# TensorE picks the width of a mixture-of-experts layer by the expert's token count

## The chip, the cores and the metric

The kernel runs on one core of a Trainium2 chip. The metric is the device time of one execution in microseconds (us), and less is better. The engines are called as in the profile: PE is TensorE (PEld its weight load), DVE is VectorE, ACT is ScalarE, POOL is GpSimd, and SP is the queue that starts most of the DMAs.

## The reference

A delta-rule attention over 4 batches, 8 heads, 768 steps and 48 features gives 3072 token rows of 384 numbers. A gate sends each token to one of 8 experts, which is two matrix products with a ReLU between them:

```python
logits = x @ w_gate                      # 3072 x 8
expert_idx = np.argmax(logits, axis=1)   # one expert for each token
for e in range(E):
    xe = x[expert_idx == e]
    h = np.maximum(xe @ w1[e], 0.0)      # 384 -> 1024
    out[expert_idx == e] = gate_w[...] * (h @ w2[e])   # 1024 -> 384
```

With the reference's inputs (seed 0) the experts 0 to 7 get 401, 342, 407, 383, 373, 410, 399 and 357 tokens.

## The kernel before, in words

**Attention.** The tokens are worked on in 24 chunks of 128. It takes a little over half of the span and is not changed.

**Routing.** Behind each chunk, `emit_slots` (L451) gives each token a slot: `base` holds the next free slot of every expert. POOL writes the token's row into the buffer `xg` in HBM with an indirect DMA (L519). An expert owns 448 slots (`CAP`): three groups of 128 and a last group of 64. At two points of the program `base` is raised for all experts (L495 and L497): behind chunk 18 to at least slot 256, behind chunk 22 to at least slot 384. So the groups in front are complete early and can be loaded early, the last group of every expert always holds the tokens of the last two chunks, and some slots in front stay empty. An empty slot is a row of zeros, and its result is dropped when it is written out. The last two chunks go to a buffer of their own, `xt`, which `load_last` (L595) loads as `xs` and `add_last` (L859, on DVE) adds to the last group.

**Experts.** For each expert `tokens` (L862) loads the 448 rows and transposes them to features by tokens in three steps (L882 for the full groups, L883 for the last one). `ffn` (L886) runs the first layer in eight blocks of 128 hidden features. A block is nine matmuls with 448 moving columns (`first`, L619: weights and tokens are each split in a high and a low part, three products for each of three slices of 128 features). ACT and DVE turn a block into the high and the low part of the hidden layer (L622, L623), and PE has three PSUM buffers for blocks. The second layer is 24 matmuls with 384 columns for each full group (`second`, L629) and 16 for the last group (L916). ACT scales the result by the gate (L911), and POOL scatters it to the output (L632). Of expert 0 the first two groups are computed during the attention, so what is left of it has 192 columns.

**Order.** The instructions of each engine stand in the order in which the loop over `t` writes them (0 to 11 for each expert: eight blocks, then the groups 0, last, 1, 2). `TOK`, `TOK0`, `PC` and `PC0` say at which `t` a step of the next expert's tokens or of its weights is written. Each engine works through its own list and waits on semaphores; SP's DMAs and POOL's scatters are lists as well.

**End.** Tokens beyond 448 of an expert would go through a loop of blocks. Behind the last expert DVE counts these blocks (L954 to L966). Each engine reads the count into a register (L975), which also waits for PE and ACT, and branches past the loop, since the count is zero here.

## Time and profile before

| | us |
|---|---|
| median of 3 runs | 563.91 |
| lowest, highest | 562.20, 567.53 |
| the profiled execution: its time | 564.33 |
| the profiled execution: its span | 562.6 |

The profile shows one execution. Its span runs from the first to the last instruction; the run's time is 1.73 us longer. Times in the rows are us from the start of the span. Line numbers such as L619 are those of the kernel before; in the next section, instruction lists headed by "now" have those of the changed file.

### The profile page before, as it was taken

What the parts mean: (1) busy time and instruction counts of PE and PEld (TensorE: products, weight loads), DVE (VectorE), ACT (ScalarE), POOL (GpSimd) and SP (SyncE); (2) the same over time, 40 slices, a digit from 0 to 9 for tenths busy, and PEclk for the clock granted to TensorE, in tenths of its full rate; (3) what the DMA queues carried; (4) which work ended last, traced back from release to release, by engine and by line L of the source; (5) the groups of instructions that cost most, each with busy time, mean ns of one, the idle gap of its engine ahead of it and who ended that gap; (6) DMA issues with size and microseconds to landing.
All of it is one profiled execution on the core that took longest, in us unless ns stands there. A gap on an engine that the chain in (4) does not pass through costs nothing.

```text
span 562.6 us, 17239 instructions
## 1 busy us (share of the span) xinstructions
PE 495.2 (88%) x7091; PEld 449.2 (80%) x7091; DVE 366.1 (65%) x1343; ACT 267.1 (47%) x590; POOL 94.6 (17%) x116
## 2 busy tenths in 40 slices
PE   5765597889989688978998999999999999999991
PEld 3554486778878677867897989999999999999991
DVE  2999989899999999746543666272744535372311
ACT  1661165576767474747342454353534435353310
POOL 4040001122421223132202010202011010202011
PEclk7996699899999998989999899999999999999996
DMA  8949449765874843655421565473745445371000
GB/s 264 289 92 267 159 152 280 212 208 155 231 248 97 267 132 118 195 170 168 154 74 71 148 213 165 114 208 108 205 122 161 131 128 166 119 201 54 12 17 25
DMA packets 68497, 88.61 MB, mean 157 GB/s; under 512 B 26541, under 2 KB 55390, under 8 KB 68416
## 3 DMA queue, kind: packets, MB, share of 16 engines
q1 hardware_dynamic: 64960, 77.92, 47.7%
q0 software_dynamic: 3456, 9.57, 4.8%
q8 instruction: 56, 0.92, 0.7%
q14 instruction: 25, 0.20, 0.1%
HBM read 57.20 MB, written 24.37 MB: 145 GB/s over the span
## 4 chain that ended last, share of the span: by engine, by line
PE 64%; DVE 27%; issue 3%; ACT 2%; DMA 1%; POOL 0%; SPq 0%; DVEq 0%; ACTq 0%; POOLq 0%
PE h L619 22%; PE y L629 18%; DVE lw L325 8%; DVE tmp L318 8%; PE y L916 4%; PE yp L404 3%; PE ks L388 3%; PE yp L422 3%; PE xp L445 2%; DVE v_all L380 2%; PE pq L235 2%; PE ks L361 2%; DVE wt L331 2%; PE ku L413 1%; PE xt L882 1%
## 5 line engine op out<-in xcount | busy, mean ns | idle before, releaser
L629 PE MATMUL y<-w2h,hx 128*128 128x384 f32 x352 | 93.5, 340 | 0.0
L325 DVE TENSOR_TENSOR lw<-lw,tmp 128x84 f32<-128x84 f32 (+26 forms) x372 | 83.7, 265 | 0.3
L318 DVE TENSOR_TENSOR tmp<-lg,lw 128x84 f32<-128x84 f32 (+26 forms) x372 | 79.9, 254 | 0.3
L552 DVE TENSOR_TENSOR w2l<-w2r,w2h 128x768 fp32r<-128x768 f32 x32 | 31.2, 978 | 73.2 <-ACT w2h L551 73.2
L392 ACT COPY u<-ks 32x384 f32<-32x384 f32 x96 | 45.1, 470 | 51.7 <-PE ks L388 50.1
L632 POOL DMA_INDIRECT out_dram<-yo,idx x32 | 30.7, 958 | 227.1 <-ACT yo L911 170.5
L629 PEld LDWEIGHTS y<-w2h,hx 128*128 128x128 f32 x352 | 63.8, 188 | 0.9
L619 PE MATMUL h<-xh,w1h 128*128 128x448 f32 x168 | 61.4, 365 | 0.0
L619 PE MATMUL h<-xh,w1l 128*128 128x448 f32 x168 | 61.3, 365 | 0.0
L619 PE MATMUL h<-xl,w1h 128*128 128x448 f32 x168 | 61.3, 365 | 0.0
L629 PE MATMUL y<-w2l,hx 128*128 128x384 f32 x176 | 59.1, 336 | 0.0
L388 PE MATMUL ks<-v_all,wt 32*32 32x48 f32 x1536 | 27.7, 211 | 35.0 <-DVE v_all L380 29.3
L388 PEld LDWEIGHTS ks<-v_all,wt 32*32 32x32 f32 x1536 | 23.2, 111 | 40.3 <-DVE v_all L380 33.1
L623 DVE SCALAR_TENSOR_TENSOR hx<-h,hx 128x448 fp32r<-128x448 f32 (+1 forms) x64 | 36.9, 587 | 24.8 <-ACT hx L622 24.4
L246 POOL TENSOR_SCALAR_AFFINE_SELECT pm<-pm 128x1024 f32<-128x1024 f32 x24 | 31.1, 1297 | 126.0 <-ACT pm L245 126.0
L622 ACT ACTIVATE hx<-h 128x448 fp32r<-128x448 f32 (+1 forms) x64 | 32.2, 515 | 38.5 <-PE h L619 38.5
L911 ACT ACTIVATE yo<-y,gt 128x384 f32<-128x384 f32 x22 | 12.8, 581 | 73.7 <-PE y L629 59.3
L361 PE MATMUL ks<-st,kt 128*32 128x96 f32 x768 | 46.5, 260 | 0.7 <-issue 0.7
L519 POOL DMA_INDIRECT xg<-row,sli x22 | 23.7, 1075 | 99.9 <-DVE sli L512 54.9
L220 ACT COPY gg<-pg 128x512 f32<-128x512 f32 x48 | 25.8, 588 | 26.3 <-PE pg L235 26.3
L361 PEld LDWEIGHTS ks<-st,kt 128*32 128x32 f32 x768 | 34.9, 115 | 4.2 <-issue 1.3
L552 DVE TENSOR_TENSOR w1l<-w1r,w1h 128x1024 fp32r<-128x1024 f32 x24 | 29.5, 1230 | 7.9 <-ACT w1h L551 7.5
(159 smaller groups left out, 1003.2 us busy)
## 6 DMA issues: line engine op xcount, KB each, us to landing
w1r<-in_w_dram SPq DMA_DIRECT2D x24, 512.0 KB, 4.0
w2r<-in_w_dram SPq DMA_DIRECT2D x32, 384.0 KB, 3.6
kt<-in_kt_dram SPq DMA_DIRECT2D x24, 256.0 KB, 5.5
qt<-in_qt_dram SPq DMA_DIRECT2D x24, 256.0 KB, 5.2
xg<-zrow SPq DMA_DIRECT2D x7, 788.0 KB, 8.0
xr<-xg SPq DMA_DIRECT2D x7, 591.0 KB, 6.0
xn<-row SPq DMA_DIRECT2D x10, 394.0 KB, 5.7
ku<-in_kn_dram SPq DMA_DIRECT2D x20, 192.0 KB, 3.4
```

Of the source, the lines that this page charges most:

```text
L246: nc.gpsimd.affine_select(out=pm, in_=pm, compare_op=ALU.is_gt, fill=0.0, base=0, pattern=[[0, H], [1, C]], channel_multiplier=-1)
L318: nc.vector.tensor_tensor(out=x, in0=lg[:, r0:r1, c:c + 1].broadcast_to([128, r1 - r0, b - a]), in1=lw[:, c:c + 1, a:b].broadcast_to([128, ...
L325: nc.vector.tensor_tensor(out=lw[:, r0:r1, a:b], in0=lw[:, r0:r1, a:b], in1=x, op=ALU.subtract)
L361: nc.tensor.matmul(ks[32 * q:32 * q + 32, 2 * p:2 * p + 2, :], lhsT=kt_t[n % KTL][:, p, 32 * q:32 * q + 32], rhs=st_view(n % B, p), start= ...
L388: nc.tensor.matmul(ks[r, h, :], lhsT=tiles[n // B]["wt"][r, n % B * H + h, :], rhs=vn[r, h, :], start=True, stop=True, tile_position=(32 * ...
L392: nc.scalar.copy(out=uview(n)[r], in_=ks[r])
L552: nc.vector.tensor_tensor(out=lo, in0=src, in1=hi.bitcast(F32), op=ALU.subtract)
L619: nc.tensor.matmul(ps, lhsT=w[:, d, fs], rhs=x_[:, d], start=(n == 0), stop=(n == len(terms) - 1))
L622: nc.scalar.activation(out=hh, in_=ps, func=AF.Relu)
L623: nc.vector.scalar_tensor_tensor(out=hl, in0=ps, scalar=0.0, in1=hh.bitcast(F32), op0=ALU.max, op1=ALU.subtract)
L629: nc.tensor.matmul(ps, lhsT=h(f)[h_], rhs=w2[w][:, f, :], start=(n == 0), stop=(n == len(terms) - 1))
L632: nc.gpsimd.indirect_dma_start(out=out, out_offset=bass.IndirectOffsetOnAxis(ap=idx, axis=0), in_=yo, in_offset=None, bounds_check=N - 1, ...
```

## The change

`emit_slots` raises `base` for expert 0 alone, and the last two chunks go to `xg` as well; `xt`, `xs` and `add_last` are gone. For the other experts `base` is then a plain count. DVE makes from it a number for each expert: 0 (at most 384 tokens), 1 (at most 416) or 2. Behind the first layer of expert 0 PE loads the seven numbers into registers, and a nest of branches stands at each of the eight blocks and at the last group of the experts 1 to 7. The nest at a block leads to nine matmuls with 384, 416 or 448 columns; the nest at the last group leads past its 16 matmuls where the number is 0. The count of the overflow blocks moves ahead of expert 0, its register load and a drain of POOL into the last expert, and the last group of the last expert is scaled by DVE and ACT, half each.

```diff
@@ emit_slots
-        dst = xg if tb * B + b < NN - DEF else xt
...
-            V.scalar_tensor_tensor(out=base, in0=lim, scalar=float(128 * NG - CAP), in1=base, op0=ALU.add, op1=ALU.max)
+            V.tensor_tensor(out=base, in0=base, in1=jump[:, 1], op=ALU.max)
...
-            nc.gpsimd.indirect_dma_start(out=dst, out_offset=bass.IndirectOffsetOnAxis(ap=sli[:, j:j + 1], axis=0),
+            nc.gpsimd.indirect_dma_start(out=xg, out_offset=bass.IndirectOffsetOnAxis(ap=sli[:, j:j + 1], axis=0),
@@ load_last
-        xs = xp_.tile([128, ROW], F32, name=f"xs{e}", tag="xs", bufs=2)
         for a in range(2):
-            nc.sync.dma_start(out=xs[64 * a:64 * a + 64], in_=xt[e * CAP + NG * 128:e * CAP + NG * 128 + 64, :])
-        return xs
+            nc.sync.dma_start(out=XR[e][64 * a:64 * a + 64, NG], in_=xg[e * CAP + NG * 128:e * CAP + NG * 128 + 64, :])
@@ tokens
-        xs = load_last(e)
...
-        add_last(xr, xs)
@@ ffn
-            first(ps[:, c], W["w1"], (xh, xl), slice(f * 128, (f + 1) * 128))
+            for i in by_width(e):
+                w = WID[i]
+                first(ps[:, c.start:w], W["w1"], (xh[..., 0:w - lo], xl[..., 0:w - lo]), slice(f * 128, (f + 1) * 128))
...
+                if (e, g) == (E - 1, NG - 1):
+                    hw = DM // 2
+                    nc.vector.tensor_scalar(out=yo[:, hw:], in0=ps[:, hw:], scalar1=gg_, scalar2=None, op0=ALU.mult)
+                    nc.scalar.activation(out=yo[:, 0:hw], in_=ps[:, 0:hw], func=AF.Copy, scale=gg_)
...
-                for n, (w_, f) in enumerate(terms):
-                    nc.tensor.matmul(ps[0:2 * w], lhsT=h2[:, f], rhs=w_[:, f, :],
-                                     start=(n == 0), stop=(n == len(terms) - 1))
+                for i in by_width(e):
+                    for n, (w_, f) in enumerate(terms if i else ()):
+                        nc.tensor.matmul(ps[0:2 * w], lhsT=h2[:, f], rhs=w_[:, f, :],
+                                         start=(n == 0), stop=(n == len(terms) - 1))
@@ new, ahead of the loop over the experts
+    for i, w in enumerate(WID[:2]):
+        V.tensor_tensor(out=kind[:, i], in0=base, in1=lim, op=ALU.subtract)
+        V.tensor_scalar(out=kind[:, i], in0=kind[:, i], scalar1=float(w - CAP), scalar2=None, op0=ALU.is_gt)
+    V.tensor_tensor(out=kind_i, in0=kind[:, 0], in1=kind[:, 1], op=ALU.add)
...
+    def by_width(e):
+
+        if e == 0:
+            yield 2
+            return
+        with tc.If(KIND[e] < 1) as low:
+            yield 0
+        with low.Else():
+            with tc.If(KIND[e] < 2) as mid:
+                yield 1
+            with mid.Else():
+                yield 2
...
@@ in the loop over the experts
+            if e == 0 and t == KF:
+                for i in range(1, E):
+                    KIND[i] = nc.values_load(kind_i[0:1, i:i + 1], engines=[mybir.EngineType.PE], min_val=0, max_val=2,
+                                             skip_runtime_bounds_check_because="a sum of two comparisons")
...
+            if e == E - 1 and t == 7:
+                nblk = nc.values_load(tot[0:1, 0:1], min_val=0, max_val=NJ + E)
+                nc.gpsimd.drain()
@@ behind the last expert: the count (cnt, nb, cum, tot and six POOL fills) is gone from here
-    nblk = nc.values_load(tot[0:1, 0:1], min_val=0, max_val=NJ + E)
     OV = tc.If(nblk > 0)
```

PE now, first layer of expert 1, the joint between two copies of a block and the next nest. In the names, `h` is the block's PSUM buffer, `xh` and `xl` are the two parts of the tokens, `w1h` and `w1l` those of the weights. The row with 384 columns is the last of the first copy:

```order
L621 MATMUL h_5696<-xh_5822,w1l_5753 128x384
L947 UNCONDITIONAL_BRANCH
L950 COMPARE_AND_BRANCH
L621 MATMUL h_5696<-xh_5822,w1h_5752 128x416 [waits Activation_49]
L621 MATMUL h_5696<-xl_5823,w1h_5752 128x416
```

Where nine matmuls of 448 columns stood, three copies of nine stand one behind the other, with branches between them that lead on to the next block.

PE, second layer of expert 1, the last group, with the transposes of the next expert's tokens (`xt`) ahead of it. Before:

```order
L882 MATMUL xt_1_6110<-ident,xr_5936 128x128 [waits PE_49]
L882 MATMUL xt_1_6110<-ident,xr_5936 128x128 x2
L883 MATMUL xt_1_6110<-ident,xr_5936 128x64
L916 MATMUL y_3_6117<-w2h_5840,hx_5940 128x384 [waits DVE_49]
L916 MATMUL y_3_6117<-w2l_5841,hx_5940 128x384
```

And now:

```order
L879 MATMUL xt_1_6298<-ident,xr_5974 128x128 [waits PE_49]
L879 MATMUL xt_1_6298<-ident,xr_5974 128x128 x2
L880 MATMUL xt_1_6298<-ident,xr_5974 128x64
L947 COMPARE_AND_BRANCH
L947 UNCONDITIONAL_BRANCH [waits PE_49]
L950 COMPARE_AND_BRANCH
L926 MATMUL y_5697<-w2h_5862,hx_5978 128x384 [waits DVE_49]
```

On the empty path nothing stands but a branch, and ahead of it PE waits for its own semaphore (`PE_49`), that is, until its matmuls up to there are finished.

POOL, the end of the program. Before:

```order
L953 IOTA e_7854 128x8 [waits PE_49]
L958 IOTA thr 128x168
L968 MEMSET itr 128x1
L969 IOTA part 128x1
L971 IOTA wo_7876 128x3
L972 IOTA wo_7877 128x8
L632 DMA out_dram<-yo_2_7808,idx_0_7433 3072x384 [waits DMASW6_49,Activation_49]
L975 TENSOR_LOAD tot [waits DVE_49,PE_49,Activation_49]
L1074 COMPARE_AND_BRANCH
```

Now:

```order
L1002 TENSOR_LOAD tot [waits DVE_49]
L947 UNCONDITIONAL_BRANCH x6
L634 DMA out_dram<-yo_0_8903,idx_0_8375 3072x384 [waits DMASW3_49,Activation_49]
L634 DMA out_dram<-yo_3_8932,idx_0_8375 3072x384 [waits DMASW4_49,DVE_49]
L634 DMA out_dram<-yo_1_8973,idx_0_8375 3072x384 [waits DMASW5_49,Activation_49]
L634 DMA out_dram<-yo_2_9002,idx_0_8375 3072x384 [waits DMASW6_49,Activation_49]
L1111 COMPARE_AND_BRANCH
```

The fills are gone from between the last scatters, and the register load stands ahead of the last four. The engines that have no part in a nest each get one unconditional branch for it, as POOL's six here.

## Rows read from the trace of the kernel before

**Rows 1.** The page: busy us (share) and instructions; the queue of PE's code.

```profile
PE 495.2 (88%) x7091; PEld 449.2 (80%) x7091; DVE 366.1 (65%) x1343; ACT 267.1 (47%) x590; POOL 94.6 (17%) x116
...
q8 instruction: 56, 0.92, 0.7%
```

**Rows 2.** Chain that ended last, experts 2, 3 and 7: start us, us, what.

```profile
361.22 14.68 PE h L619 x72
375.90 0.33 PE xt L882 x3
376.23 0.20 PE xt L883
376.43 4.39 PE y L629 x24
380.82 0.33 PE xt L882 x3
381.15 0.20 PE xt L883
381.35 2.98 PE y L916 x16
...
384.86 8.52 PE y L629 x48
393.39 14.42 PE h L619 x72
...
535.92 4.18 PE y L629 x24
540.09 2.77 PE y L916 x16
```

**Rows 3.** Busy us (x) of PE, PEld, DVE, ACT, POOL; PE clock, DMA share, GB/s.

```profile
100.00:200.00 100.00, 86.88 (x2264) 76.65 (x2262) 93.90 (x457) 68.14 (x193) 22.93 (x20) 0.98 0.68 197
...
380.00:420.00 40.00, 40.00 (x220) 37.73 (x219) 19.40 (x30) 17.67 (x29) 5.72 (x6) 1.00 0.49 141
```

**Rows 4.** Timeline, the end: start us, us, engine, line, operation [idle before <-releaser].

```profile
550.85 0.34 PE L629 MATMUL y<-w2h,hx 128*128 128x384 f32 x1
551.27 0.14 POOL L953 IOTA e<- 128x8 f32 x1 [2.33 <-PE y L629]
551.28 0.58 ACT L911 ACTIVATE yo<-y,gt 128x384 f32<-128x384 f32 x1 [3.58 <-PE y L629]
...
551.44 0.17 DVE L954 TENSOR_TENSOR cnt<-base,e 128x8 f32<-128x8 f32 x1 [7.25 <-POOL e L953]
...
552.25 0.99 POOL L632 DMA_INDIRECT out_dram<-yo,idx  x1 [0.17 <-issue]
...
554.07 0.15 DVE L966 CAST tot<-cum 128x1 int32<-128x1 f32 x1
```

**Rows 5.** Timeline, expert 0's rest and the attention's last steps.

```profile
294.60 0.86 PE L388 MATMUL ks<-v_all,wt 32*32 32x48 f32 x16
...
306.27 0.97 POOL L519 DMA_INDIRECT xt<-row,sli  x1 [0.30 <-issue]
...
308.18 0.92 PE L619 MATMUL h<-xb,w1h 128*128 128x192 f32 x2 [0.41 <-ACT xb L551]
...
309.25 2.37 SPq L598 DMA_DIRECT2D xs<-xt  x4
...
311.12 0.36 DVE L623 SCALAR_TENSOR_TENSOR hx<-h,hx 128x192 fp32r<-128x192 f32 x1 [2.60 <-ACT hx L622]
...
319.59 0.49 PE L882 MATMUL xt<-ident,xr 128*128 128x128 f32 x3
320.01 0.27 PE L883 MATMUL xt<-ident,xr 64*128 64x64 f32 x1
```

**Rows 6.** DMA issues: queue, operation and count, KB each, median us to landing.

```profile
xs<-xt SPq DMA_DIRECT2D x16, 98.5 KB, 2.4
...
out_dram<-yo,idx POOLq DMA_INDIRECT x32, 2.6
```

**Rows 7.** As rows 3, around the start of expert 0's rest.

```profile
304.00:308.00 4.00, 2.53 (x21) 2.22 (x20) 1.21 (x8) 0.78 (x2) 1.94 (x2) 1.00 0.18 68
308.00:312.00 4.00, 3.82 (x17) 3.72 (x18) 0.72 (x2) 1.37 (x3) 0.00 (x0) 0.51 0.31 90
312.00:316.00 4.00, 4.00 (x25) 4.00 (x25) 2.08 (x4) 1.85 (x5) 0.00 (x0) 0.64 0.88 251
```

## The prediction, written before the changed kernel ran

> **What bounds the kernel now.** I read the page's first part, then the chain of waits behind 330 us, then the table of stretches, then the timeline of the end. The page gives PE 88% of the span, DVE 65% and ACT 47% [rows 1]; a share over the whole span does not say who is waited for. The chain does: through the experts it holds nothing but PE, one piece end to end with the next [rows 2]. An expert is 72 matmuls of the first layer (14.42 or 14.68 us), three sets of transposes, 24 matmuls of group 0, 16 of the last group and 48 of the groups 1 and 2, about 32 us. [...] So each us taken from PE there is a us of the span, until DVE or DMA, at half load, come into the way. Behind PE's last matmul (550.85 + 0.34 = 551.19 us) the end of the program takes 562.6 - 551.19 = 11.4 us: POOL's fills, the count on DVE to 554.22, then 8.4 us with no instruction that the profile shows, in which the register load, the branch and the closing barriers lie [rows 4].

> **Which way the branches go.** The tokens of an expert, from the reference, are also the values that the changed `base` holds for the experts 1 to 7, since these are no longer raised. 342, 383, 373 and 357 (experts 1, 3, 4, 7) are kind 0: 384 columns and no last group. 407, 410 and 399 (experts 2, 5, 6) are kind 1: 416 columns. Expert 0 is not branched.

> **A. Narrower first layer.** A matmul of 448 columns takes 14.42/72 = 200.3 ns (14.68/72 = 203.9 where the expert's number is even). One of 384 columns takes 4.18/24 = 174.2 ns in the last expert, 8.52/48 = 177.5 and 4.39/24 = 182.9 in a loaded one [rows 2]. The difference is at most 203.9 - 174.2 = 29.7 ns and at least 200.3 - 182.9 = 17.4. [...] That is 72 x 26 = 1.87 us for kind 0 and half, 0.94, for kind 1: 4 x 1.87 + 3 x 0.94 = 10.3 us (6.9 to 11.8).

> **B. The skipped last group.** Three times 2.98 us and once 2.77 [rows 2]: 11.7 us. On the empty path PE waits until its own transposes are finished, so it runs dry four times. What that costs no row shows. At least 0. At most 0.6: a transpose's 0.27 us [rows 5] from start to end, and the 0.30 that POOL took between two of its instructions with nothing to wait for [rows 5]. I take 0.3, the restart alone, since most of a transpose is hidden by the one behind it: 4 x 0.3 = 1.2 us back (0 to 2.4).

> **C. The branches.** There are 7 x 9 = 63 nests. Kind 0 runs one comparison and one jump, kind 1 two comparisons, a jump over the first copy and one over the third. They cost PE nothing if its sequencer is ahead. The small matmuls of the attention pass at 0.86/16 = 54 ns each [rows 5], so nine are handed over in 0.49 us or less, while nine of 384 columns run for 9 x 174 = 1.57 us: 1.1 us a block is free. And ahead of each expert's first transposes the sequencer has waits on DMAs to pass, ahead of the second set it has none of these; both sets take 0.33 + 0.20 us [rows 2]. An instruction that the sequencer handles alone left no mark on PE. Below nothing I see no reason for; the upper bound is a fetch of code at each jump, at the 2.4 us of the fastest DMA landing [rows 6], which is a rival below. I take 0 by the nearest row, the waits.

> The row on those waits says that control work is free. [...]

> **D. Seven register loads on PE** behind expert 0's first layer. Not in any row. At least 0, at most one round trip of 2.4 us, the fastest DMA landing [rows 6], since they stand one behind the other and PE still has queued matmuls of 192 columns. I take 0.

> **E. The end.** The 3.03 us from PE's end to the count (551.19 to 554.22) leave the path, and so does the register load behind it. What is late next is the last scatter: half the scaling on each of two engines saves about 0.2 us of ACT's 0.58, so it starts at about 552.0 instead of 552.25 and lands 2.6 us later [rows 4, 6], at 554.6 on the old clock. So the gain is the register load and the early branch, less 0.4 us. Bounds: nothing, and the 8.4 us without an instruction less the 2.6 us of that landing, 5.8. I take 2, from a load of the size of the 2.4 us landing.

> **F. What hides.** Gone are eight DVE adds, 16 loads of `xs` and eight fills of `xt`: nothing on the path, since PE never waits there [rows 2, 3]. Moved onto DVE ahead of expert 0's rest are five operations for the kinds and twelve for the count, at about 0.2 us each 3.8 us (the twelve took 551.44 to 554.22 [rows 4]). DVE is idle for 2.6 us up to 311.12 there [rows 5], so its first `hx` comes about 1 us late, and PE needs that buffer only at the fourth block, about 314; if that cover goes, 1 us. The last two scatters now also wait for expert 0's loads from `xg`, and all expert loads for both scatters, as `xs` did. SP's load of expert 1's rows comes two DMAs earlier in its list than before, with `xs` gone. The 63 plain branches on DVE, ACT, POOL and SP cost those lists little, and these engines have half their time free [rows 3].

> **The sum** is -10.3 - 11.7 + 1.2 - 2 = -22.8 us against the profiled execution: 564.33 - 22.8 = **541.5 us**. The median before, 563.91, is 0.4 us below that execution, within what runs differ. The kindest ends of all terms give 564.33 - 11.8 - 11.7 - 5.8 = 535.0, the worst 564.33 - 6.9 - 11.7 + 2.4 + 2.4 + 1 = 551.5.

> **Rivals.**

> *Slower: code is fetched at each jump.* [...] For: the queue of PE's code brought 56 packets for 0.92 MB, about 253 of PE's 14,182 instructions each (0.7% of 16 x 562.6 us over 56 is 1.1 us a packet) [rows 1]. At 2.4 us a jump, a kind-0 block takes 0.49 + 2.4 = 2.9 us instead of 1.57, a kind-1 block with two jumps 5.3 instead of 1.68: 32 x 1.3 + 24 x 3.6 = 128 us, and with the gain of 24 us (the sum without B's restarts) 564.33 - 24 + 128 = 668 us. It decides from about 1.1 us a jump on, where 24 x (0.49 + 2.2 - 1.68) = 24 us eat the whole gain. Against: a jump passes at most 18 matmuls with their weight loads and two branches, 38 instructions, so it stays in the packet or goes to the one behind it, which was due next. [...] Chance 0.10, most of it slower.

> *No change: a branch drains PE.* If each nest, and not the empty path alone, lets the array run dry, it costs 63 x 0.3 = 19 us: 564.33 - 24 + 19 = 559 us; at 0.6, 578. For: a register is compared, and nothing says what is held meanwhile. Against: the waits passed unseen in C. Chance 0.11.

> *The clock falls.* [...] Against: between 100 and 200 us PE rests 13% of the time in small pieces, and the clock stays at 0.98 [rows 3]; the new pauses are smaller and fewer. Chance 0.04.

> *The branch takes the wide path*, for counts other than those I worked out: only the end gains, 562 us. Chance 0.02.

> **How the numbers follow.** The forecast has 0.73. Its own range is 535 to 551.5; with the clock's case and part of a draining branch I give 535 to 555, which leaves out the fetch, the full drain and the wide path, under 0.2. A difference under 1% (5.6 us) can't be told from none. Faster by more: 0.73, the clock's 0.04 and a small part of the draining branch, 0.79. Same: most of the draining branch, the wide path and the fetch near its balance, 0.12. Slower: 0.09.

> **What would show it.** In the profile after: blocks of 72 matmuls of 12.5 us in the experts 1, 3, 4 and 7 and of about 13.5 in 2, 5 and 6; no matmuls of the last group in four experts; PE at 9 tenths and more through the experts, with a gap of about 0.3 us where the group is skipped; about 9.4 us from PE's last matmul to the end. I am wrong if PE shows gaps at the joints of the blocks that its sequencer is named for (C), if the gap at an empty group is 1 us or more (B), if PE stops at 315 to 320 for its registers (D), or if the end still takes 11 us (E).

## The result and the profile after

| | before | after |
|---|---|---|
| median of 4 runs each, us | 563.06 | 540.81 |
| lowest, highest | 559.93, 567.53 | 539.12, 543.51 |
| the profiled execution: time, span | 564.33, 562.6 | 543.51, 541.8 |

The ratio of the runs is 0.960 (95% interval 0.953 to 0.968): faster, by 22.2 us. The forecast was 541.5.

I cut both profiled spans at the same places: the start of expert 0's rest, its end, the start of the transposes behind it, PE's last end.

| stretch, us | before | after | difference |
|---|---|---|---|
| attention, up to expert 0's rest | 308.18 | 311.06 | +2.9 |
| expert 0's rest, first layer | 11.41 | 10.32 | -1.1 |
| pause of PE behind it | 0 | 1.31 | +1.3 |
| from there to PE's last matmul | 231.60 | 213.40 | -18.2 |
| from PE's last matmul to the end | 11.4 | 5.7 | -5.7 |
| span | 562.6 | 541.8 | -20.8 |

The first two lines can't be put down to the change. Attention's code is nearly the same, yet in 14 profiled executions of the kernels of this study expert 0's rest began anywhere from 303.45 to 316.00 us, in the two with the old layout at 308.18 and 308.15, and the rest itself took 10.3 to 11.8. So kernels are compared below by the stretches behind it.

The page (as [rows 1]):

```profile
PE 481.1 (89%) x7027; PEld 440.0 (81%) x7027; DVE 361.9 (67%) x1341; ACT 268.2 (49%) x590; POOL 96.1 (18%) x119
...
q8 instruction: 66, 1.08, 0.8%
```

PE runs 64 matmuls less, the four empty groups, and ten packets of code more, the copies.

The first layers of the experts 1 to 7 after, one stretch each (from:to, length, busy us and count of PE, then of PEld, clock, DMA share, GB/s), matmuls of the first layer alone:

```profile
331.80:345.00 13.20, 13.04 (x72) 12.35 (x72) 1.00 0.75 247
360.00:374.00 14.00, 13.72 (x72) 13.47 (x72) 1.00 0.69 199
391.20:404.20 13.00, 12.64 (x72) 12.50 (x72) 1.00 0.63 190
419.00:432.00 13.00, 12.65 (x72) 12.51 (x72) 1.00 0.64 202
447.00:461.30 14.30, 14.07 (x72) 13.44 (x72) 1.00 0.64 201
478.60:492.60 14.00, 13.72 (x72) 13.48 (x72) 1.00 0.61 189
509.80:522.80 13.00, 12.65 (x72) 12.50 (x72) 1.00 0.05 18
sum 94.50, PE 92.51 PEld 90.23; mean PE 13.22 PEld 12.89
```

The same view of before, its sum:

```profile
sum 105.00, PE 103.39 PEld 94.08; mean PE 14.77 PEld 13.44
```

Each busy figure holds 0.16 us of the last matmul's end, which the chain of [rows 2] gives to the next piece: 14.58 here is 14.42 there. The experts 1, 3, 4 and 7 run the narrowest of a block's three copies, 2, 5 and 6 the middle one, and the layers take 10.9 us less in all (103.39 - 92.51). In the 40 us of [rows 3] at 380, in which PE had been busy throughout and DVE and the DMA engines for about half, PE still has hardly a gap:

```profile
380.00:420.00 40.00, 39.57 (x227) 38.46 (x226) 18.39 (x29) 17.78 (x31) 6.45 (x7) 1.00 0.45 148
```

The 0.43 us that are missing in these 40 are the pause at one empty group. Timeline of PE there:

```profile
408.87 0.49 PE L879 MATMUL xt<-ident,xr 128*128 128x128 f32 x3
409.29 0.27 PE L880 MATMUL xt<-ident,xr 64*128 64x64 f32 x1
409.99 0.55 PE L879 MATMUL xt<-ident,xr 128*128 128x128 f32 x3 [0.43 <-PEq L947]
```

PE's waits, in total, times, longest: those that are new.

```profile
PE xt L879 <- PEq L947: 1.5, 3, 0.5
PE xt L879 <- issue: 1.3, 1, 1.3
PE y L631 <- PEq L947: 0.4, 1, 0.4
```

The sequencer's branch (PEq L947) ends four pauses, one at each empty group; no pause stands at a joint of two blocks. The single wait of 1.3 us is that for the seven registers. Timeline of PE around it (`L621` is expert 0's rest):

```profile
321.11 0.27 PE L621 MATMUL h<-xb,w1l 128*128 128x192 f32 x1
...
322.69 0.52 PE L879 MATMUL xt<-ident,xr 128*128 128x128 f32 x3 [1.31 <-issue]
```

The end (as [rows 4]):

```profile
535.76 0.33 PE L631 MATMUL y<-w2h,hx 128*128 128x384 f32 x1
536.13 0.42 DVE L917 TENSOR_SCALAR yo<-y,gt 128x192 f32<-128x192 f32 x1 [7.34 <-PE y L631]
536.63 0.42 ACT L918 ACTIVATE yo<-y,gt 128x192 f32<-128x192 f32 x1 [4.11 <-DVEq L1111]
537.33 0.97 POOL L634 DMA_INDIRECT out_dram<-yo,idx  x1 [2.40 <-ACTq L1111]
```

The two halves of the last scaling run one behind the other (ACT's is released from DVE), 536.13 to 537.05, 0.92 us where ACT alone had taken 0.58. Behind the end of the last scatter's issue only 3.5 us are left; they were 9.4 [rows 4]. Apart from the count on DVE before, no engine works in them, but POOL's queue has rows there: the program closes with three drains on POOL, and the first is the longest. Count, then ns of the shortest, the middle and the longest, then when the first and the last start; before and after:

```profile
L1108 POOLq DRAIN  x3: 40/107/4648, 557.1 to 562.4; - x3
L1145 POOLq DRAIN  x3: 46/107/386, 540.2 to 541.5; - x3
```

This closing drain took 4.65 us before and takes 0.39 now. The chain also has the drain that the change puts into the last expert, where POOL had nothing else to do:

```profile
510.90 0.51 POOLq L1002
511.41 0.70 POOL out_dram L634
512.11 4.32 POOLq L1003
```

### The profile page after: what moved, and what is told of

It reads as the page before. It is cut to its first block, busy times and chain, and to the rows that moved or that the text cites. A ratio compares the mean times of both kernels' runs of the same rounds, so it can differ in the third digit from the quotient of the medians.

```text
span 541.8 us, 17275 instructions
## 1 busy us (share of the span) xinstructions
PE 481.1 (89%) x7027; PEld 440.0 (81%) x7027; DVE 361.9 (67%) x1341; ACT 268.2 (49%) x590; POOL 96.1 (18%) x119
## 5 line engine op out<-in xcount | busy, mean ns | idle before, releaser
L324 DVE TENSOR_TENSOR tmp<-lg,lw 128x84 f32<-128x84 f32 (+26 forms) x372 | 78.7, 251 | 0.3
L621 PE MATMUL h<-xh,w1h 128*128 128x384 f32 (+1 forms) x168 | 57.7, 343 | 0.0
L621 PE MATMUL h<-xl,w1h 128*128 128x384 f32 (+1 forms) x168 | 57.6, 343 | 0.0
L621 PE MATMUL h<-xh,w1l 128*128 128x384 f32 (+1 forms) x168 | 57.5, 342 | 0.0
L394 PE MATMUL ks<-v_all,wt 32*32 32x48 f32 x1536 | 29.2, 210 | 29.7 <-DVE v_all L386 24.7
L524 POOL DMA_INDIRECT xg<-row,sli x24 | 25.8, 1075 | 97.0 <-DVE sli L517 43.0
L241 PE MATMUL pg<-kt 64*128 64x128 f32 x384 | 30.2, 291 | 6.1 <-ACT gg L226 3.6
```

The lines of the kernel that those rows point to most:

```text
L324: nc.vector.tensor_tensor(out=x, in0=lg[:, r0:r1, c:c + 1].broadcast_to([128, r1 - r0, b - a]), in1=lw[:, c:c + 1, a:b].broadcast_to([128, ...
L394: nc.tensor.matmul(ks[r, h, :], lhsT=tiles[n // B]["wt"][r, n % B * H + h, :], rhs=vn[r, h, :], start=True, stop=True, tile_position=(32 * ...
L621: nc.tensor.matmul(ps, lhsT=w[:, d, fs], rhs=x_[:, d], start=(n == 0), stop=(n == len(terms) - 1))
```

## The experiments

**What the end gained from: e1_no_drain, e2_late_load, e3_before_drain.** I had put the end's gain down to the register load; the drain had no term.

```diff
 e1: the changed kernel
-                nc.gpsimd.drain()
 e2: the changed kernel
-                nblk = nc.values_load(tot[0:1, 0:1], ...)     # in the last expert
+    nblk = nc.values_load(tot[0:1, 0:1], ...)                 # behind the last expert
 e3: the kernel before, in the loop over t
+            if e == E - 1 and t == 7:
+                nc.gpsimd.drain()
```

> The changed kernel without the drain of POOL in the last expert; count and register load stay early. From PE's last matmul to the end of the span the kernel before took 11.4 us and the changed one 5.7, where I had forecast 9.4. Theory (the drain): the 4.3 us that the drain took at 512 us would otherwise be taken behind the last scatter, so the end goes from 5.7 back to about 10 us and the time from 540.8 to about 545. Rival (the register load and the count were the whole of it): the end stays at 5.7 us and the time at 540.8.

> The changed kernel with the register load of the overflow count put back behind the last expert; the count on DVE and the drain of POOL stay early. Theory (the drain carries most of the 5.7 us): the load costs about the 1.3 us in which PE took seven such loads, or less, so PE's last matmul to the end goes from 5.7 to at most 7. Rival (the load, which waits for PE and ACT and makes every engine wait, carries it): the end goes to about 9 to 10 us.

> The kernel before with one thing added: a drain of POOL in the last expert, ahead of its last scatters. Count and register load stay at the end. Theory (the drain): from PE's last matmul to the end falls from 11.4 to about 7 us, by the 4.3 us that the drain took in the changed kernel; the rest of the kernel reads as before. Rival (count and register load): the end stays at 11.4 us.

PE's last matmul and the last scatter of e1:

```profile
536.46 0.33 PE L631 MATMUL y<-w2h,hx 128*128 128x384 f32 x1
...
538.03 0.97 POOL L634 DMA_INDIRECT out_dram<-yo,idx  x1 [2.43 <-ACTq L1110]
```

and of e2:

```profile
540.80 0.34 PE L631 MATMUL y<-w2h,hx 128*128 128x384 f32 x1
...
542.60 0.97 POOL L634 DMA_INDIRECT out_dram<-yo,idx  x1 [2.67 <-ACTq L1111]
```

and of e3, where the count on DVE still ends at 552.92:

```profile
549.56 0.34 PE L629 MATMUL y<-w2h,hx 128*128 128x384 f32 x1
...
550.95 0.99 POOL L632 DMA_INDIRECT out_dram<-yo,idx  x1 [0.17 <-issue]
...
552.77 0.15 DVE L968 CAST tot<-cum 128x1 int32<-128x1 f32 x1
```

The spans end at 547.4, 547.4 and 556.4. From PE's last end that is 10.6 us without the drain (about 10 expected), 6.3 with a late load (at most 7), and 6.5 in the kernel before with a drain alone (about 7; 11.4 without). The drain carries 4.9 us whichever kernel it stands in; load, count and halves together 0.8. The closing drain goes the same way: its row has 4.65 us in e1 and 0.39 in e2 and e3, which is 4.3 of the 4.9; what makes up the rest is not shown. In the runs e1 is 544.65 us (ratio to before 0.968, 0.962 to 0.974), against an expected 545; e2 and e3 ran once each and are read by their traces alone.

**Does the drain pay for what came before it? e11_drain_half.**

```diff
+            if e == 3 and t == 7:
+                nc.gpsimd.drain()
             if e == E - 1 and t == 7:
                 nblk = nc.values_load(...)
-                nc.gpsimd.drain()
```

> The changed kernel with the drain of POOL moved from the last expert to the fourth, so that 16 of the 56 indirect DMAs come behind it instead of four. Without a drain PE's last matmul to the end is 10.6 us, with the drain in the last expert 5.7. Theory (a drain works off what was issued since the one before): end 5.7 + 4.9 x 12/52 = 6.8 us, and the early drain takes less than 4.3 us. Rival (the first drain of a program costs 4 to 5 us whatever came before): 5.7 us. Rival (what counts is only that the last DMAs but four are confirmed): 10.6 us.

PE's last matmul and the last scatter of e11 (span 536.4), then the drain itself, POOL's scatter that runs beside it, and the closing drain (drains as above):

```profile
529.05 0.33 PE L631 MATMUL y<-w2h,hx 128*128 128x384 f32 x1
...
530.62 0.97 POOL L634 DMA_INDIRECT out_dram<-yo,idx  x1 [2.43 <-ACTq L1112]
```

```profile
L1002 POOLq DRAIN  x1: 4327/4327/4327, 385.6 to 385.6; - x1
...
385.79 0.97 POOL L634 DMA_INDIRECT out_dram<-yo,idx  x1 [3.24 <-ACT yo L920]
...
L1146 POOLq DRAIN  x3: 46/107/1692, 533.9 to 536.2; - x3
```

The end is 7.0 us, 6.8 expected. The expectation had miscounted, though: the drain stands ahead of the fourth expert's own scatters, so four scatters for each of five experts come behind it, 20 and not 16, and 36 stand in front; with 20 the same sum gives 7.2. With 4, 20 and 56 indirect DMAs since the last drain the ends are 5.7, 7.0 and 10.6, so it is those behind the drain that are paid at the end, some 0.08 to 0.09 us for each. The closing drain shows it directly: 0.39, 1.69 and 4.65 us, 0.08 for each. The drain in the middle fits too. Its row (4.33 us) begins while a scatter still runs; behind that scatter's end it takes some 3.1 us with 36 DMAs in front, where the changed kernel's took 4.32 with 52, and that of e3, in the kernel before, 4.7 by the same cut. So the early drain was shorter, as expected.

**The price of the branches alone: e4_wide_copies.**

```diff
-                w = WID[i]
+                w = CAP
...
-                    for n, (w_, f) in enumerate(terms if i else ()):
+                    for n, (w_, f) in enumerate(terms):
```

> The changed kernel with all three copies of a block 448 columns wide and with the last group computed for every number: all branches, counts and register loads stay, only the work saved is put back. Theory (branches are hidden, A and B are nothing but matmul time): the first layer of the experts 1 to 7 is back at 14.4 to 14.7 us with no gaps at the joints, the pauses of 0.4 to 0.55 us at the empty groups are gone since there is no empty path, and the time is that of the changed kernel plus 10.9 (first layer) plus 11.5 - 2.4 (last groups less restarts) = 20 us, about 561. Rival (the branches cost PE something that the narrower matmuls' trace can't show, 0.05 us at each of 63 nests): first layer 0.4 us above that in each expert, time about 564. Rival (the branches help, or the saved columns also made other matmuls quicker): below 558.

First layers of the experts 1, 2 and 3, and the sum over all seven, as above:

```profile
330.00:346.00 16.00, 15.12 (x72) 13.35 (x72) 1.00 0.72 225
362.00:378.00 16.00, 14.75 (x72) 13.51 (x72) 1.00 0.52 168
395.00:411.00 16.00, 14.56 (x72) 13.50 (x72) 1.00 0.57 172
...
sum 112.00, PE 103.07 PEld 94.29; mean PE 14.72 PEld 13.47
```

103.07 against 103.39 before: 56 nests at the blocks cost PE nothing. From expert 0's second layer to PE's last matmul it takes 232.31 us, 19.6 more than the changed kernel's 212.75 (20.0 expected). In the runs it is 559.54 us, 0.993 of before (0.990 to 0.996): what is left is the end's gain less the register loads, -5.7 + 1.3 = -4.4 us, or 0.992.

**No control at all: e5_no_branch.**

```diff
-        with tc.If(KIND[e] < 1) as low:
-            yield 0
...
+        yield (2, 0, 1, 0, 0, 1, 1, 0)[e]
...
-            if e == 0 and t == KF:
-                for i in range(1, E):
-                    KIND[i] = nc.values_load(...)
```

> The changed kernel with the numbers of the experts fixed in the program, as these inputs give them: no branches and no register loads on PE; each block stands once, with its 384 or 416 columns, and the empty groups are not written at all. It is no replacement for the kernel, since the counts are data. Theory (the control costs the pauses the trace shows and nothing else): the 1.31 us ahead of expert 1's transposes go, and so do the four pauses of 0.43 to 0.55 us with their slower restart; the first layers stay at 12.5 to 12.9 and 13.6 to 13.9 us. Time 540.8 - 1.3 - 2.0 to 2.4 = about 537.3. Rival (the second layer's matmuls, 0.1 us a group slower after the change, are slow because of the branches too): 8.43 us for two groups again instead of 8.57, another 1 us less in all. Rival (branches cost more than the pauses): first layers below 12.4 us.

Measured 537.83 us (about 537.3 expected), 0.951 of before (0.948 to 0.955). All five pauses are gone, and the stretch from expert 0's second layer to PE's last matmul is 210.27 us, 2.5 less than with branches: 0.6 us for each of the four empty groups, restart and all. (Five kernels with the same work, the changed one, e1, e2, e7 and e11, differ by 0.7 us in this stretch, so the 0.6 holds to about 0.2.) The first layers stay at 12.5 to 12.8 and 13.6 to 13.9. So do the 8.55 us for two groups of the second layer (8.43 before, by the same cut): that slowness does not come from branches. Its matmuls take 342 and 338 ns instead of 340 and 336 from start to modelled end, 528 of them 1.1 us; the cause is open.

**Loads spread out: e6_spread_whole; and the scatters: e12_last_first.** Both scale the last group on ACT alone.

```diff
-            if e == 0 and t == KF:
-                for i in range(1, E):
-                    KIND[i] = nc.values_load(kind_i[0:1, i:i + 1], engines=[PE], ...)
+            if e + 1 < E and t == (KF if e == 0 else 4):
+                KIND[e + 1] = nc.values_load(kind_i[0:1, e + 1:e + 2], engines=[PE], ...)
 e12 besides:
-        for g in (0, NG, 1, 2) if e > 0 else
+        for g in ((0, NG, 1, 2) if e < E - 1 else (NG, 0, 1, 2)) if e > 0 else
```

> The changed kernel with the seven register loads of PE spread out, one in each expert behind its fourth block, and the last group scaled by ACT alone. Theory (the 1.31 us are seven loads of 0.19 us one behind the other with the matmuls' queue empty; one load alone is covered by queued matmuls; the two halves of the scaling write one buffer and run one behind the other, 0.92 us against 0.58): no gap of 1.3 us ahead of expert 1, no gap above 0.2 us behind a fourth block, the end 0.3 us shorter than 5.7; 1.3 + 0.3 = 1.6 us less, about 539.2. Rival (any register load lets PE run dry, whatever stands in front of it): a gap of 0.4 us or more in each expert, seven of them, 2.8 us instead of 1.3, about 542.

> The kernel with the spread register loads and the scaling on ACT alone, and in the last expert the order last group, 0, 1, 2 instead of 0, last, 1, 2. In the kernel with the spread loads the last scatter began 0.86 us behind ACT's scaling, where 0.28 is usual: the last expert's scatters each wait for the one before to land, and the scatter of its empty group stood in that row. Theory (that row of scatters sets the end): the last scatter begins 0.28 us behind the scaling, PE's last matmul to the end 6.0 - 0.6 = 5.4 us; with the 1.3 us of the register loads 1.6 us under the changed kernel, about 539.2. Rival (the end is set by the closing barriers, not the scatter): 6.0 us, about 539.8.

In e6 no pause is left for any register load: the 1.31 us are gone, and the six later loads leave no mark. But the end is 6.0 us, not shorter. Its last rows:

```profile
531.66 0.97 POOL L634 DMA_INDIRECT out_dram<-yo,idx  x1 [1.85 <-DMA out_dram<-yo,idx]
533.92 0.58 ACT L915 ACTIVATE yo<-y,gt 128x384 f32<-128x384 f32 x1 [3.66 <-PEq L1105]
535.36 0.97 POOL L634 DMA_INDIRECT out_dram<-yo,idx  x1 [2.72 <-DMA out_dram<-yo,idx]
```

ACT is done at 534.50; the scatter starts 0.86 us later and is released by the scatter before it. PE skips the empty group, but POOL still scatters it, and each of these waits for the one before. With the empty group first (e12, PE's last end 534.16, span 539.5):

```profile
534.20 0.58 ACT L915 ACTIVATE yo<-y,gt 128x384 f32<-128x384 f32 x1 [3.60 <-PE y L631]
535.07 0.97 POOL L634 DMA_INDIRECT out_dram<-yo,idx  x1 [3.22 <-ACTq L1105]
```

The scatter follows ACT by 0.29 us, and the end is 5.3 us (5.4 expected). In the runs e6 is 542.16 us (0.960 of before, 0.957 to 0.963), e12 540.33 (0.956, 0.952 to 0.961), the changed kernel 0.960 (0.953 to 0.968). For both 539.2 was expected. e6's time is the one that its rival gave, 542, but the rival's gap in each expert is not in the trace. By the traces e12 is 1.5 us better than the changed kernel behind the attention (1.3 of loads and 0.4 of the end, less a pause that was 0.13 longer); the runs cannot tell that from none.

**The rival that would have been slower: e7_near_jump, e9_jump_54, e10_jump_90, e8_far_jump.** These inputs never run the third copy in the experts 3 and 4, so lengthening it changes only how far their 16 jumps go (k is 1, 4, 8 and 16).

```diff
                 first(ps[:, c.start:w], W["w1"], ...)
+                for _ in range(k if e in (3, 4) and i == 2 else 0):
+                    first(ps[:, c.start:w], W["w1"], ...)
```

> The changed kernel with the third copy of each block of the experts 3 and 4, the one with 448 columns, lengthened by nine matmuls. These inputs never run that copy there (both experts run the first), so PE's work is unchanged, and each of 16 jumps passes 27 matmuls instead of 18. It is the control for the next kernel. All theories: the first layers of the experts 3 and 4 stay at 12.5 us, time as the changed kernel.

> As the kernel with 27 matmuls under a jump, but with the copy that is never run lengthened by 144 matmuls instead of nine: each of the 16 jumps of the experts 3 and 4 passes 162 matmuls, some 324 instructions, more than the 253 that a packet of PE's code holds. Rival of the prediction (code is fetched at a jump whose target is not at hand): a fetch of 1.1 us (a packet's time) to 2.4 us (a DMA's landing) at each jump, with 0.49 us to hand over the next block; a block goes from 1.57 to between 1.6 and 2.9 us, the first layers of the experts 3 and 4 from 12.5 to between 13 and 23 us each, with gaps at the joints of the blocks; time 541.5 to 562. Theory of the prediction if jumps cost nothing whatever they pass: 12.5 us, as the control.

> As the kernel with 162 matmuls under a jump in the experts 3 and 4, but with 54: 108 instructions, under half a packet of PE's code. With 162 the two first layers took 26.95 and 33.51 us instead of 12.5: the first three blocks ran without a pause, then pauses of 0.25 to 4.94 us. Theory (PE's code comes in order, skipped or not, at 3.4 to 4.2 us for the 1.4 packets of a block there, 2.5 to 3 us a packet): with 54 a block is half a packet, 1.2 to 1.5 us, under the 1.57 us of its matmuls; nothing is lost, 12.5 us each. Rival (each jump costs a fetch by itself): 2.2 us a jump as with 162 matmuls, 12.5 + 17 us each. Rival (a price by packets with no cover): 4.6 packets more at 2 us, 4.5 us in each of the two experts.

> The same with 90 matmuls under a jump, 180 instructions; a block is 0.8 of a packet of code. Theory (code in order at 2.5 to 3 us a packet): 2.0 to 2.4 us a block against 1.57 us of matmuls, so after the blocks that were at hand 0.4 to 0.8 us are lost in each; 2 to 6 us in each of the two experts, 14.5 to 18.5 us. Rival (only a jump whose target lies more than a packet away stalls): 12.5 us. Rival (each jump costs a fetch by itself): some 30 us.

| matmuls under a jump | 18 (changed) | 27 (e7) | 54 (e9) | 90 (e10) | 162 (e8) |
|---|---|---|---|---|---|
| first layer of expert 3, to the next piece, us | 12.48 | 12.49 | 12.63 | 19.08 | 26.95 |
| of expert 4 | 12.49 | 12.48 | 14.05 | 20.10 | 33.51 |
| packets of PE's code | 66 | 67 | 70 | 75 | 84 |
| time of the run, us | 543.51 | 543.34 | 546.43 | 559.45 | 582.47 |

The largest pause of e8, and the stretches around it (columns as [rows 3]):

```profile
443.60 0.34 PE L621 MATMUL h<-xh,w1l 128*128 128x384 f32 x1
448.88 0.68 PE L621 MATMUL h<-xh,w1h 128*128 128x384 f32 x1 [4.94 <-issue]
```

```profile
440.00:444.00 4.00, 2.75 (x15) 2.12 (x13) 2.02 (x3) 1.51 (x3) 0.62 (x1) 1.00 0.84 223
444.00:448.00 4.00, 0.00 (x0) 0.00 (x0) 0.62 (x1) 0.52 (x1) 0.00 (x0) 0.98 0.93 256
448.00:452.00 4.00, 2.28 (x6) 1.78 (x6) 0.00 (x0) 0.00 (x0) 0.00 (x0) 0.50 0.03 9
```

PE stands still between two blocks, waiting for nothing that the profile shows, while the DMA engines are 84 and 93% busy; from 448 us on the granted clock is 0.50 in the 4 us that the last row covers. The first pause of e10 comes behind the fourth block of expert 3:

```profile
397.05 0.62 DVE L625 SCALAR_TENSOR_TENSOR hx<-h,hx 128x448 fp32r<-128x448 f32 x1 [0.81 <-ACT hx L624]
...
399.21 0.34 PE L621 MATMUL h<-xh,w1l 128*128 128x384 f32 x1
401.57 0.43 PE L621 MATMUL h<-xh,w1h 128*128 128x384 f32 x1 [2.02 <-DVE hx L625]
```

The DVE step that the last row names had long been done: the fifth block takes the buffer of the second, and DVE had read that by 397.67 (first row). So here too no engine is left that PE could have waited for.

The stall that the rival stands for is real, and it is not a price for each jump: in e10 four blocks of expert 3 and five of expert 4 pass before the first pause, in e8 three and one, and 54 matmuls under a jump cost 0.1 us in expert 3 and 1.6 in expert 4, where nothing had been expected. e8 lost more than the rival's own upper bound (23 us a layer, 562 in all). Code that is jumped over is brought all the same. Beyond e7's, e9, e10 and e8 hold 864, 2016 and 4320 instructions more under their jumps, 3.4, 8.0 and 17.1 packets of 253, and the page counts 3, 8 and 17 more. So the account that fits is the code of a whole block against its matmuls' 1.57 us: 0.8 packets took 2.4 us a block (e10), 1.4 packets 3.8 us (e8), an estimate of about 3 us a packet for these two runs, the data DMAs and the lower clock of e8's rows above included. That was the theory ahead of e10; its 2 to 6 us in each expert were somewhat low (6.6 and 7.6). A block of the changed kernel is 27 matmuls and four branches, some 58 instructions, 0.23 of a packet, or 0.7 us at that pace.

A jump in e10 passes 180 instructions, less than a packet of 253, and the two layers lost 14 us all the same; so the rival that only a farther target stalls, at 12.5 us a layer, fails too. That the packets come in order is an assumption of this account: the page counts them and gives no order.

## Why the prediction was right, and where its sizes were not

**A, narrower first layer:** -10.9 us measured, -10.3 taken. The 26 ns a matmul in the forecast's sum are the difference of the quiet rows, 200.3 - 174.2. They were the right ones: 174.2 ns were taken for 384 columns, and the layers of the experts 3, 4 and 7 give 12.49 / 72 = 173.5. The 0.6 us more come from the experts 1 and 4, whose layers had taken 14.95 and 14.68 before, where the quiet 14.42 was taken for all.

**B, the skipped group:** 11.5 us of matmuls gone, as taken (11.7). The restart was mis-sized: pauses of 0.43 to 0.55 us, 0.6 each with the slower start behind them, 2.5 us in all instead of 1.2, just over the upper bound of 2.4. A transpose's own 0.27 us, which I held hidden, would fill the difference; that was not tried.

**C, 63 nests at nothing:** right (e4, 103.07 us against 103.39), and e8 to e10 fit the reason given, that the sequencer is ahead. By them what that rests on is the code of a block: 0.23 packets in the changed kernel, 0.8 where 6.6 and 7.6 us were lost. The rival's ground for its low chance, that short jumps stay near, was right in effect; its price of 2.4 us a jump was the wrong form.

**D, seven register loads at nothing:** wrong. PE's queue ran empty for 1.31 us, 0.19 a load. My bound of 2.4 held it, but I let queued matmuls cover all seven, and they did so only for one at a time (e6).

**E, the end:** right in sign, -5.7 instead of -2, near its bound of 5.8, and the step's reason failed. I gave the 8.4 us without an instruction to the register load, "from a load of the size of the 2.4 us landing"; the runs put 4.9 us on the drain, which stood in the change and in no term, and 0.8 on all the rest. The trace of before already had the answer: in those 8.4 us stands the closing drain of 4.65, in the rows of POOL's queue that I had not read. The halves did not save 0.2 us; one behind the other they cost 0.3.

**F:** nothing of it showed on the path. One thing was missing: the empty group's scatter stays in POOL's row and is at the edge of the end (e6, e12).

**The sum:** -10.9 - 11.5 + 2.5 + 1.3 - 5.7 = -24.3, and about 1.1 us of slower second layer back, -23.2; the stretches behind the attention give 1.3 - 18.2 - 5.7 = -22.6, the runs -22.2. The forecast of -22.8 was so near by luck: E was 3.7 us too small, and B, D and the second layer were 3.7 us too kind. The clock did not fall at the empty groups: it is 1.00 from 330 us to PE's end.

## What to carry to other kernels

The branches at the blocks cost PE nothing here (e4, 103.07 us against 103.39). By e8 to e10 I expect that as long as all the code up to the next block, the skipped part too, comes in faster than the engine works through the taken part: here an estimated 0.7 us of code against 1.57 us of matmuls. Load the registers one at a time behind queued work (e6: no pause, against 1.31 us for seven in a row). A path that skipped work on the busiest engine let that engine run dry once, 0.6 us each time (e5), so it should skip more than that, as the 2.8 to 3.0 us of a last group here, and the other engines' share of the skipped work is still there (e6: the last scatter 0.86 us behind ACT, against 0.29 in e12). At an end in which no engine works, read the rows of the queues, ask which one still has something to confirm, and try a drain where that engine is idle (4.9 us here, e1).
